# Re-cutting the head of a fused attention and Fourier kernel into ten segments, with GpSimd splits and two cycles for each of the last output tiles

## The chip, the cores and the metric

The kernel runs on one core of a Trainium2 chip. The metric is device time in microseconds (us), the median over runs of the whole kernel. Engines are named as the profile names them: PE (TensorE matmul) and PEld (its weight loads), DVE (VectorE), ACT (ScalarE), POOL (GpSimd), SP (SyncE, which here only issues DMAs).

## The reference

```python
def reference(A_x, A_wqkv, A_wo, B_x, B_dft_seq_re, B_dft_seq_im, B_dft_hid_re, B_dft_hid_im, gate_w):
    x = A_x                                              # (1, 2048, 640), 32 heads of 20
    g = _sigmoid((x * gate_w).sum(-1, keepdims=True))
    # a: attention
    qkv = (x @ wqkv).reshape(B, S, 3, H, Dh).transpose(2, 0, 3, 1, 4)
    q, k, v = qkv[0], qkv[1], qkv[2]
    scores = jnp.einsum("bhqd,bhkd->bhqk", q, k) * (Dh ** -0.5)
    a = jnp.einsum("bhqk,bhkd->bhqd", _softmax(scores), v) ... @ wo
    # b: real part of a DFT over hidden, then over sequence
    ar = jnp.einsum("bsd,ed->bse", x, dft_hid_re)
    ai = jnp.einsum("bsd,ed->bse", x, dft_hid_im)
    b = jnp.einsum("ts,bse->bte", dft_seq_re, ar) - jnp.einsum("ts,bse->bte", dft_seq_im, ai)
    return g * a + (1 - g) * b
```

## The kernel before

Everything is float32. Matmuls run on pairs of a rounded part and a remainder: `split` writes the rounded copy with one engine and the remainder (a subtract) with another, and a product takes three matmuls (`three`). The schedule is written out by hand: instructions stand on each engine in the order in which the program makes them, and tiles rotate through fixed numbers of buffers (five PSUM banks `ps` from `bank()`, five `pair_tile`s, three `raw_tile`s, three `part_tile`s). Stores are collected in a list and issued on SP by `flush(keep)`, which leaves the `keep` youngest for later.

**Head.** First come the projections. 40 q/k tiles (`qk_tile(c, t)`: 15 matmuls of 512 columns into one bank, a split from PSUM into a pair tile by ACT and DVE, and a store of 512 KB to DRAM) and the v tiles; then 32 of the q/k tiles, eight column blocks of four, with **segments** between them. A segment (`segment(i, steps)`, before the first tile of each block, eight in all) interleaves two other jobs:

- one hidden tile (`hid_tile`): one block of the DFT over the hidden dimension, 15 yields of two 64-row matmuls that run beside each other in the two halves of the array, into the banks `yp0` and `yp1`, then read by ACT (L357) and DVE (L358) and stored to `a_scr`;
- five score steps (`run_s`, `s_mm`, L167): per step two matmuls (two heads) of 512 scores, each followed by a DVE maximum (L169). The softmax needs the row maxima ahead of the exponentials; a head start of `LEAD = 41` steps is made here: eight segments of five steps, and one step at the end. After step 31 the first unit's maxima are gathered (`max_nm`), and after step 33 they are transposed (`max_chain`, L201).

Inside a segment each step is followed by three hidden yields.

**Main loop.** 256 cycles, each of which follows the string `ORDER`: eight scores `e` (L844, then an ACT exponential, L846), eight scores `m` for the maxima 41 steps ahead, 15 places `F` for fill, and at the end a burst `B` of 16 attention-times-v matmuls (L518) for the two key tiles of this cycle. The fill is a chain of generators, and `goals` says how far it is to be at each place: first the hidden tiles that the head has not made (64 less `HEAD`, so 56, one per cycle, L349), then 56 units of the DFT over the sequence, three cycles each (L599), then `out_tile`, the output product over the first four of five blocks of `wo` for the 16 row tiles, two halves each, one half per cycle (L670). That fills 56 + 168 + 32 = 256 cycles. The maxima run out 41 steps (ten cycles) before the end.

GpSimd makes the splits of the main loop, combines transfers, scales and adds the DFT result `y` to the output (`add`, L686 and L687), and normalises the attention output. Its `load_pre(tt)` brings a row tile of the attention output for `out_tile`. `LAST` holds what is loaded in the last ten steps: the fifth block of the first eight row tiles (`load_o4`) and the part of it that is known for the other eight (`load_old`).

**Tail.** After the last burst the last unit's attention output is normalised: `spread`, four `recip`, a product, four DMAs (`move`), `split_last`. Meanwhile `short_row(tt)` adds the fifth block for row tiles 0 to 7: six matmuls, a DVE or ACT+POOL addition per half, and the store of the row tile. After `split_last` the same is done for tiles 8 to 15.

Of the kernel before, what the change touches and what calls it, by code (L numbers as in the profile page):

```python
# [11 lines left out]
R = mybir.dt.float32r  # L12
AF = mybir.ActivationFunctionType
ALU = mybir.AluOpType
# [4 lines left out]
P = 128  # L19
S = 2048  # L20
D = 640
H = 32
DH = 20
ND = D // P
# [14 lines left out]

LEAD = 41  # L40

HEAD = 8

# [11 lines left out]


LONG = (0, 0, 0, 0, 0, 0, 0)
FULL = 0  # L60
PRE = range(FULL, NS)
UNITS = len(PRODUCTS) * HT

# [3 lines left out]
def f32(ap):  # L67
    return ap.bitcast(F32)
# [3 lines left out]
def mix_kernel(ctx: ExitStack, tc: tile.TileContext, xa, wqk, wb, cdft, wo, out):  # L72
    nc = tc.nc
    pe, act, dve, pool, sp = nc.tensor, nc.scalar, nc.vector, nc.gpsimd, nc.sync
# [16 lines left out]
    y_scr = dram.tile([NS, P, D], F32, name="y_scr")  # L91
    r_scr = dram.tile([NU, 4, 512], F32, name="r_scr")
    l_scr = dram.tile([NU, 4, 512], F32, name="l_scr")
    o_scr = dram.tile([D, S], F32, name="o_scr")
# [10 lines left out]
    ngate = const.tile([P, NS], F32, name="ngate")  # L105

    def split(dst1, dst2, src, e1, e2):
        if e1 is act:
            act.activation(dst1, src, AF.Copy)  # L109
        else:  # L110
            e1.tensor_copy(dst1, src)  # L111
        e2.tensor_tensor(dst2, src, f32(dst1), op=ALU.subtract)  # L112

    def three(ps, st1, st2, mv1, mv2, first, last):
        pe.matmul(ps, st1, mv1, start=first, stop=False)  # L115
        pe.matmul(ps, st1, mv2, start=False, stop=False)  # L116
        pe.matmul(ps, st2, mv1, start=False, stop=last)  # L117
# [3 lines left out]
    def bank():  # L121
        return ps_w.tile([P, 512], F32, name=f"ps{next(turn) % 5}")

    def pair_tile():
        return work.tile([P, 2, 512], F32, name="p", bufs=5)

    def raw_tile():
        return work.tile([P, 1024], F32, name="raw", bufs=3)

    def part_tile():  # L130
        return work.tile([P, 2, 1024], R, name="part", bufs=3)
# [21 lines left out]
    def at_step(i, fn):  # L153
        later.setdefault(i, []).append(fn)
# [103 lines left out]
    def idle(n):  # L258
        ps = bank()
        for _ in range(n):  # L260
            pe.matmul(ps, zeros[:, :P], zeros, start=True, stop=True)
# [27 lines left out]

        return finish  # L290

    stores = []

    def flush(keep=0):
        while len(stores) > keep:
            sp.dma_start(*stores.pop(0))

    def qk_tile(c, t):
        w = wt[c]
        ps = bank()  # L300
        x1, x2 = xs[0][t], xs[1][t]
        for d in range(ND):
            if (c, t) == (0, 0) and d > 0:
                if d == 1:
                    idle(3)
                pe.matmul(ps, w[:, 0, d], x1[:, d], start=False, stop=False)
                pe.matmul(ps, w[:, 1, d], x1[:, d], start=False, stop=False)
                pe.matmul(ps, w[:, 0, d], x2[:, d], start=False, stop=d == ND - 1)
            else:
                three(ps, w[:, 0, d], w[:, 1, d], x1[:, d], x2[:, d], d == 0, d == ND - 1)  # L310
        st = pair_tile()
        split(st[:, 0].bitcast(R), st[:, 1].bitcast(R), ps, act, dve)
        stores.append((qk_scr[:, t, c * P : (c + 1) * P].rearrange("z p c -> p z c"), st))
        flush(2)

    def mm_b(j, s, ps, n):
        w = wt["b", j]
# [46 lines left out]
    def segment(i, steps):  # L364
        def read_out(read, args):
            read()
            stores.append(args)

        tile_ = hid_tile(i, read_out)
        left = 3 * ND  # L370
        for k in range(steps):
            run_s(step + 1)
            for _ in range(left // (steps - k)):
                next(tile_)
                left -= 1

    step = 0

    def run_s(upto):
        nonlocal step  # L380
        while step < upto:
            s_step(step)
            step += 1
# [22 lines left out]
    for s in range(12, 16, 2):  # L406
        v_pair(0, s)
    fin()
    hid_done = 0
    order = [1, ND + 1, 2, ND + 2, 3, ND + 3, 4, ND + 4]  # L410
    for s in range(0, NS, 2):
        v_pair(1, s)
# [8 lines left out]
    for n, c in enumerate(order):  # L421
        for t in range(4):
            m = 4 * n + t
            if m % 4 == 0 and hid_done < HEAD:
                segment(hid_done, 5)
                hid_done += 1
            qk_tile(c, t)
            if t == 1:
                if n + 1 < len(order):
                    fin()  # L430
                if n + 2 < len(order):
                    fin = load_wqk(order[n + 2])
# [135 lines left out]
    signs = {}  # L568
    st = {(th * HT + t, hf): 0 for th in range(2) for t in range(HT) for hf in range(2)}
# [73 lines left out]
    def load_o4():  # L643
        raw = raw_tile()[:, : (HT - FULL) * P]
        sp.dma_start(raw, o_scr[(ND - 1) * P :, FULL * P : HT * P])
        at_step(total - 4, functools.partial(finish_o4, raw))

    def finish_o4(raw):
        o = part_tile()[:, :, : (HT - FULL) * P]
        split(o[:, 0], o[:, 1], raw, pool, pool)  # L650
        for t in range(FULL, HT):
            o4[t] = o[:, :, (t - FULL) * P : (t - FULL + 1) * P]

# [79 lines left out]
    ops = {}  # L733


    def make_sel():
# [3 lines left out]
            pool.tensor_copy(sel[:, 32 * j : 32 * j + 32], ident[:, c : c + 1].to_broadcast([P, 32]))  # L740
        chain.append(sel)

    total = 32 * NU
    LAST = {total - 10: load_o4, total - 9: load_old}
    done = 0
    goals = {}
    def read_later(read, args):
        extras.append((now[0], read))
        at_step(now[0] + 2, functools.partial(sp.dma_start, *args))

    HID = 4 * NS - HEAD
    fills = itertools.chain(*(hid_tile(HEAD + g, read_later) for g in range(HID)), itertools.chain.from_iterable(dft_step(g) for g in range(NS * UNITS)),
                            itertools.chain.from_iterable(out_tile(tt, hf) for tt in PRE for hf in range(2)))
# [5 lines left out]
    first = start // 4  # L759
    last = total // 4 - 1  # L760
    cycles = [(c, c + 1, 3 * ND) for c in range(HID)]
    edge = [first]
    for u in range(UNITS):
        k, t = LONG[u // HT], u % HT
        edge.append(edge[-1] + 3 + k * (t + 1) // HT - k * t // HT)
    cycles += [(edge[u], edge[u + 1], 3 * NS) for u in range(UNITS)]
    cycles += [(edge[-1] + u, edge[-1] + u + 1, 3 * (ND - 1)) for u in range(2 * len(PRE))]
    assert cycles[-1][1] <= last + 1
    at_goal = 0
    for c0, c1, count in cycles:  # L770
# [4 lines left out]
            at_goal += share  # L775

    for k, tt in enumerate(PRE):
        i = 4 * (edge[-1] + 2 * k)

        def load(tt=tt, i=i):  # L780
            at_step(i - 6, load_pre(tt))

        at_step(i - 11, load)
# [24 lines left out]
    def end(i):  # L808
        if i % 4 == 2:
            c = i // 4  # L810
            if c + HEAD in (NS, 2 * NS):
                at_step(i + 2, load_wb(3 + (c + HEAD) // NS, pool, pool))
            if c in (HID - 18, HID - 17, HID - 16):
# [5 lines left out]
            if c in (HID - 7, HID - 5, HID - 3):  # L819
                at_step(i + 4, load_c((c - HID + 7) // 2))  # L820
        if i in LAST:
            LAST[i]()

# [52 lines left out]
            fn()  # L876


    def out_half(tt, hf, y, ops, add, shared=False):
        ps = bank()[:, :HE]  # L880
        for k, (o1, o2, d) in enumerate(ops):
            w = wos[d, hf]
            three(ps, o1, o2, w[:, 0], w[:, 1], k == 0, k == len(ops) - 1)
        ye = y[:, hf * HE : (hf + 1) * HE]
        g = gate[:, tt : tt + 1]
        if shared:
            m = apool[0].tile([P, HE], F32, name="m", bufs=2)
            act.activation(m, ps, AF.Copy, scale=g)
            pool.tensor_tensor(ye, ye, m, op=ALU.add if add else ALU.subtract)
        else:  # L890
            dve.scalar_tensor_tensor(ye, ps, g, ye, op0=ALU.mult, op1=ALU.add if add else ALU.subtract)  # L891

    def short_row(tt, shared=False):
        for hf in range(2):
            out_half(tt, hf, yo[tt], [(o4[tt][:, 0], o4[tt][:, 1], ND - 1)], True, shared and hf == 1)
        sp.dma_start(out[tt * P : (tt + 1) * P, :], yo[tt])

    sel, o, rb = chain

# [9 lines left out]
    def move():  # L909
        for qc in range(2):  # L910
            for h in range(2):
                j = 2 * qc + h
                r = OLD + DH * h
                sp.dma_start(tip[0][r : r + DH, 512 * qc : 512 * qc + 512], o[32 * j : 32 * j + DH, :])  # L914

    def split_last():
        p = part_tile()
        for qc in range(2):
            c = slice(512 * qc, 512 * qc + 512)
            split(p[:, 0, c], p[:, 1, c], tip[0][:, c], act, dve)  # L920
        for t in range(HT):
            o4[HT + t] = p[:, :, t * P : (t + 1) * P]

    flush()
    short = list(range(FULL, HT))
    short_row(short[0])
    sums = spread()
    recip(sums, 0)
    for k, tt in enumerate(short[1:]):
        short_row(tt, k < 6)  # L930
        if k < 3:
            recip(sums, k + 1)
        if k == 3:
            dve.tensor_tensor(o, o, rb, op=ALU.mult)  # L934
            move()
    split_last()
    for tt in range(HT, NS):
        short_row(tt, False)

# [34 lines left out]
```

## Time and profile before

| | us |
|---|---|
| median of three runs | 1891.3 (1890.16 to 1892.07) |
| the profiled execution | 1889.33 |
| its span, first to last instruction | 1887.5 |
| head with segments | about 106 to 268 |
| hidden tiles in the main loop | 268 to 620 |
| DFT over the sequence | 620 to 1685 |
| output tiles | 1685 to 1862 |
| tail | 1862 to 1887.5 |

The stage borders are read from the matmul timeline. A row of the timeline gives start, duration, engine, line of the kernel, operation, tiles, shape and count; a bracket at its end holds the idle time of the engine before it and what ended it. A row of the waits gives the waiting instruction, what it waited for, total us, times, and the longest. A row of the groups ends in busy us, mean ns, idle time before. Back-to-back instructions overlap in the timeline (a matmul's end is modelled, and an exponential's 0.6 us contains the start of the next), so a pace is read from starts.

### The profile page before, as it was taken

The page shows a single profiled execution, that of the slowest core. Times are in us where ns is not written, and L with a number is a line of the kernel's source. Part 1 is how long each engine was busy: PE and PEld are TensorE (multiplying, and loading weights), DVE is VectorE, ACT ScalarE, POOL GpSimd, SP SyncE. Part 2 cuts the span into 40 slices and gives each one's busy share as a digit, 9 for nine tenths or more (in the row PEclk, how much of TensorE's full clock was granted, in tenths as well). Part 3 has the DMA queues.
Part 4 walks back from the last instruction along what each step waited for, and adds up shares of the span by engine and source line. Part 5 has one row for each costly group of instructions (what it writes and reads, how often), then busy time and mean ns, then how long its engine had stood idle before and what let it go on. Part 6 is the DMA issues. An engine that isn't in the chain of part 4 may idle for free. (4 is left out here: it accounts for less than half of the span.)

```text
span 1887.5 us, 44579 instructions
## 1 busy us (share of the span) xinstructions
PE 1875.0 (99%) x17477; PEld 1359.6 (72%) x17477; DVE 1471.1 (78%) x2448; ACT 1219.1 (65%) x2351; POOL 1007.0 (53%) x875
## 2 busy tenths in 40 slices
PE   9999999999999999999999999999999999999998
PEld 8987777676767676777767676777767676766666
DVE  4145469898989888888888888888888888889954
ACT  4221147777777676676767676766767676677784
POOL 1200001010035798466699899867779989634443
PEclk9999999999999999999999999999999999999999
DMA  7843341221415574636567576646485747342224
GB/s 232 179 135 133 123 148 48 65 72 50 120 45 155 167 230 148 169 119 180 175 172 243 164 250 189 170 145 185 135 250 192 217 161 213 120 114 62 61 56 151
DMA packets 174468, 280.50 MB, mean 149 GB/s; under 512 B 44095, under 2 KB 106559, under 8 KB 174259
## 3 DMA queue, kind: packets, MB, share of 16 engines
q1 hardware_dynamic: 173299, 275.69, 48.1%
q0 software_dynamic: 960, 1.97, 0.5%
q8 instruction: 137, 2.24, 0.5%
q14 instruction: 72, 0.59, 0.1%
HBM read 213.37 MB, written 63.52 MB: 147 GB/s over the span
## 5 line engine op out<-in xcount | busy, mean ns | idle before, releaser
L169 DVE TENSOR_REDUCE mx<-ps 128x1 f32<-128x512 f32 x2048 | 1294.0, 683 | 174.6 <-PE ps L167 153.8
L846 ACT ACTIVATE p<-ps 128x512 f32<-128x512 f32 x2048 | 1086.9, 599 | 432.7 <-PE ps L167 226.2
L167 PE MATMUL ps<-kst,qst 60*128 60x512 f32 x2048 | 790.2, 415 | 2.8 <-DVE p L112 0.5
L844 PE MATMUL ps<-qst,kst 62*128 62x512 f32 x2048 | 699.5, 413 | 0.2
L599 PE MATMUL yp<-x,part 64*128 64x320 f32 x5376 | 644.9, 307 | 0.0
L599 PEld LDWEIGHTS yp<-x,part 64*128 64x128 f32 x5376 | 580.1, 186 | 7.3
L518 PE MATMUL av<-p,v 128*21 128x512 f32 x4096 | 490.3, 596 | 0.0
L844 PEld LDWEIGHTS ps<-qst,kst 62*128 62x128 f32 x2048 | 336.2, 185 | 198.4 <-DVE mx L169 182.4
L167 PEld LDWEIGHTS ps<-kst,qst 60*128 60x128 f32 x2048 | 372.3, 184 | 22.7 <-DVE mx L169 9.8
L112 POOL TENSOR_TENSOR part<-raw,part 128x1024 fp32r<-128x1024 f32 (+1 forms) x129 | 290.3, 2250 | 10.3
L518 PEld LDWEIGHTS av<-p,v 128*21 128x21 f32 x4096 | 98.1, 100 | 225.6 <-issue 223.4
L349 PE MATMUL yp<-wb,x 64*128 64x320 f32 x1920 | 239.1, 308 | 0.0
L111 POOL CAST part<-raw 128x1024 fp32r<-128x1024 f32 (+1 forms) x129 | 127.1, 985 | 165.3 <-PE yp L599 154.9
L349 PEld LDWEIGHTS yp<-wb,x 64*128 64x128 f32 x1920 | 207.5, 186 | 4.0 <-DVE raw L358 0.2
L475 POOL TENSOR_TENSOR raw<-raw,raw 128x1024 f32<-128x1024 f32 x77 | 185.4, 2408 | 27.8 <-DMA raw<-in_cdft 22.2
L548 POOL TENSOR_TENSOR o<-o,rb 128x512 f32<-128x512 f32 x31 | 40.2, 1296 | 181.4 <-DMA rb<-r_scr 145.9
L111 POOL CAST wb<-raw 128x966 fp32r<-128x966 f32 (+1 forms) x4 | 3.4, 857 | 223.5 <-PE yp L349 223.5
L112 DVE TENSOR_TENSOR p<-ps,p 128x512 fp32r<-128x512 f32 x40 | 27.4, 690 | 92.5 <-ACT p L109 92.5
L670 PE MATMUL yp<-x,part 64*128 64x320 f32 x768 | 95.1, 309 | 0.0
L115 PE MATMUL ps<-x,part 128*128 128x512 f32 (+1 forms) x228 | 89.3, 392 | 2.6 <-ACT part L109 2.5
L112 POOL TENSOR_TENSOR x<-araw,x 128x320 fp32r<-128x320 f32 x96 | 83.8, 873 | 7.7
L117 PE MATMUL ps<-x,part 128*128 128x512 f32 (+1 forms) x228 | 87.8, 385 | 0.0
(80 smaller groups left out, 1174.7 us busy)
## 6 DMA issues: line engine op xcount, KB each, us to landing
raw<-in_cdft SPq DMA_DIRECT2D x192, 512.0 KB
araw<-a_scr SPq DMA_DIRECT2D x176, 160.0 KB
qk_scr<-p SPq DMA_DIRECT2D x40, 512.0 KB
kst<-qk_scr SPq DMA_DIRECT2D x90, 160.0 KB
qst<-qk_scr SPq DMA_DIRECT2D x90, 160.0 KB
a_scr<-raw SPq DMA_DIRECT2D x64, 160.0 KB
yt<-y_scr SPq DMA_DIRECT2D x64, 160.0 KB
y_scr<-yt SPq DMA_DIRECT2D x64, 160.0 KB
```

The source lines that it names most:

```text
L111: e1.tensor_copy(dst1, src)
L112: e2.tensor_tensor(dst2, src, f32(dst1), op=ALU.subtract)
L115: pe.matmul(ps, st1, mv1, start=first, stop=False)
L167: pe.matmul(ps, q[b : b + KROWS, qt * P : (qt + 1) * P], k[b : b + KROWS, kc * 512 : (kc + 1) * 512], start=True, stop=True)
L169: return lambda: dve.tensor_reduce(mx[n][:, h, qt, kc : kc + 1], ps, axis=AX.X, op=ALU.max)
L349: pe.matmul(yp[h][:, :HE], xs[xz][t][r, d, cs], w[r, wz, d, :HE], start=d == 0 and z == 0, stop=d == ND - 1 and z == 2)
L475: pool.tensor_tensor(raws[0], raws[0], raws[1], op=ALU.add if PRODUCTS[n][0][1][0] > 0 else ALU.subtract)
L518: pe.matmul(av[32 * j : 32 * j + DH + 1, :], v[:, kt, h * (DH + 1) : (h + 1) * (DH + 1)], pp[qc][:, h, :], start=kt == 0, stop=kt == NS - 1)
L599: pe.matmul(yp[h][:, :HE], c[r, cz, cs], a[r, az], start=s == 0 and z == 0, stop=s == NS - 1 and z == 2)
L670: pe.matmul(yp[h][:, :HE], o[r, oz, d], wos[d, hf][r, wz], start=d == 0 and z == 0, stop=d == ND - 2 and z == 2)
L844: pe.matmul(pt, k[b : b + KROWS + 2, kt * P : (kt + 1) * P], q[b : b + KROWS + 2, qc * 512 : (qc + 1) * 512], start=True, stop=True)
L846: act.activation(pts[n, kt, qc][:, h], pt, AF.Exp, scale=float(DH) ** -0.5)
```

## The change

`HEAD` goes from 8 to 10, and `segment` is called with four steps instead of five, before every third q/k tile instead of every fourth; `FILL` puts no hidden yields behind the first step, eight behind the second, seven behind the third and none behind the fourth. From the first segment on, `qk_tile` copies its bank out with ACT into half of a pair tile, GpSimd makes both parts of the split from there, and one store is kept back instead of two. In the main loop 54 hidden tiles remain. `FULL = 1` takes row tile 0 out of the output fill; 30 halves remain, and the last four (`SLOW`) get two cycles each, so that 54 + 168 + 26 + 8 = 256. Row tile 0 is made in the tail with all five blocks (`full_half`, 15 matmuls a half), its attention rows loaded eight steps before the end (`load_o`) and split on GpSimd two steps before the end, its `y` loaded and scaled there. Its short row goes.

```diff
-HEAD = 8
+FILL = {4: (0, 8, 7, 0)}
+HEAD = 10
...
-FULL = 0
+FULL = 1
+SLOW = 4
...
 def qk_tile(c, t):
...
+        if hid_done:
+            if not halves:
+                raw = pair_tile()
+                halves.extend((raw[:, 1], raw[:, 0]))
+            raw = halves.pop()
+            act.activation(raw, ps, AF.Copy)
         st = pair_tile()
-        split(st[:, 0].bitcast(R), st[:, 1].bitcast(R), ps, act, dve)
+        st1, st2 = st[:, 0].bitcast(R), st[:, 1].bitcast(R)
+        if hid_done:
+            split(st1, st2, raw, pool, pool)
+        else:
+            split(st1, st2, ps, act, dve)
         stores.append((qk_scr[:, t, c * P : (c + 1) * P].rearrange("z p c -> p z c"), st))
-        flush(2)
+        flush(1 if hid_done else 2)
...
 def segment(i, steps):
...
-        left = 3 * ND
-        for k in range(steps):
+        for n in FILL[steps]:
             run_s(step + 1)
-            for _ in range(left // (steps - k)):
+            for _ in range(n):
                 next(tile_)
-                left -= 1
...
-            if m % 4 == 0 and hid_done < HEAD:
-                segment(hid_done, 5)
+            if m % 3 == 0 and hid_done < HEAD:
+                segment(hid_done, 4)
                 hid_done += 1
...
+    def load_o(tt):
+        raw = raw_tile()[:, : ND * P].rearrange("p (d c) -> p d c", d=ND)
+        sp.dma_start(raw, o_scr[:, tt * P : (tt + 1) * P].rearrange("(d p) c -> p d c", p=P))
+
+        def finish():
+            o = part_tile().rearrange("p z c -> p (z c)")[:, : 2 * ND * P].rearrange("p (z d c) -> p z d c", z=2, d=ND)
+            split(o[:, 0], o[:, 1], raw, pool, pool)
+            ops[tt] = o
+
+        return finish
...
-    LAST = {total - 10: load_o4, total - 9: load_old}
+    LAST = {total - 10: load_o4, total - 9: load_old, total - 8: lambda: fins.append(load_o(0)), total - 2: lambda: fins.pop()()}
...
-    cycles += [(edge[-1] + u, edge[-1] + u + 1, 3 * (ND - 1)) for u in range(2 * len(PRE))]
+    at_tile = edge[-1]
+    for u in range(2 * len(PRE)):
+        n = 2 if u >= 2 * len(PRE) - SLOW else 1
+        cycles.append((at_tile, at_tile + n, 3 * (ND - 1)))
+        tiles.append(at_tile)
+        at_tile += n
...
+    def load_y(tt):
+        ys[tt] = pair_tile().rearrange("p z c -> p (z c)")[:, :D]
+        sp.dma_start(ys[tt], y_scr[tt])
+
+    def scale_y(tt):
+        pool.tensor_scalar(ys[tt], ys[tt], ngate[:, tt : tt + 1], 1.0, op0=ALU.mult, op1=ALU.mult)
...
+    def full_half(tt, hf):
+        o = ops[tt]
+        out_half(tt, hf, ys[tt], [(o[:, 0, d], o[:, 1, d], d) for d in range(ND)], signs[tt, hf] > 0)
+        if hf:
+            sp.dma_start(out[tt * P : (tt + 1) * P, :], ys.pop(tt))
...
     flush()
+    for tt in range(FULL):
+        load_y(tt)
     short = list(range(FULL, HT))
...
             move()
+            scale_y(0)
+    full_half(0, 0)
     split_last()
+    full_half(0, 1)
     for tt in range(HT, NS):
         short_row(tt, False)
```

More of the change, by code (lines that the diff above doesn't have):

```diff
@@ L290, in load_wb @@
         return finish
-    stores = []
+    stores, halves, hid_done = [], [], 0
     def flush(keep=0):
@@ L408, in mix_kernel @@
     fin()
-    hid_done = 0
     order = [1, ND + 1, 2, ND + 2, 3, ND + 3, 4, ND + 4]
@@ L741, in make_sel @@
         chain.append(sel)
+    def load_o(tt):
[6 more added lines that the diff above has]
+        return finish
     total = 32 * NU
-    LAST = {total - 10: load_o4, total - 9: load_old}
+    LAST = {total - 10: load_o4, total - 9: load_old, total - 8: lambda: fins.append(load_o(0)), total - 2: lambda: fins.pop()()}
     done = 0
-    goals = {}
+    goals, fins = {}, []
     def read_later(read, args):
@@ L761, in mix_kernel @@
     cycles = [(c, c + 1, 3 * ND) for c in range(HID)]
-    edge = [first]
+    edge, tiles = [first], []
     for u in range(UNITS):
@@ L777, in mix_kernel @@
     for k, tt in enumerate(PRE):
-        i = 4 * (edge[-1] + 2 * k)
+        i = 4 * tiles[2 * k]
         def load(tt=tt, i=i):
@@ L876, in mix_kernel @@
             fn()
+    ys = {}
+    def load_y(tt):
[3 more added lines that the diff above has]
+        pool.tensor_scalar(ys[tt], ys[tt], ngate[:, tt : tt + 1], 1.0, op0=ALU.mult, op1=ALU.mult)
     def out_half(tt, hf, y, ops, add, shared=False):
```

## The prediction

> **What bounds the kernel now.** I read the page's busy times first, then the span cut by stage, then inside each stage what the matmul engine (PE) waits for, and last the timelines of one segment, one cycle and the tail.
>
> ```profile
> PE 1875.0 (99%) x17477; PEld 1359.6 (72%) x17477; DVE 1471.1 (78%) x2448; ACT 1219.1 (65%) x2351; POOL 1007.0 (53%) x875
> ```
> ```profile
> 106.10:268.20 162.10, 158.75 (x854) 123.82 (x853) 86.47 (x142) 32.87 (x58) 0.00 (x0) 1.00 0.37 131
> 268.20:620.20 352.00, 352.00 (x3483) 250.59 (x3481) 316.63 (x536) 259.60 (x512) 56.68 (x59) 1.00 0.29 84
> ...
> 1822.70:1862.40 39.70, 39.70 (x400) 24.15 (x398) 10.03 (x19) 33.45 (x67) 22.58 (x27) 1.00 0.29 85
> 1862.40:1887.50 25.10, 17.84 (x100) 15.84 (x98) 17.30 (x33) 5.03 (x9) 5.87 (x7) 0.93 0.56 216
> ```
> Columns of the second fence: window, length, then PE, weight load, DVE, ACT and POOL busy, granted clock, DMA. The rows are the segments with the q/k tiles, the 56 hidden cycles, the cycles without maxima, and the tail. PE sets the pace until the tail, but 99% is a modelled figure: in the segments it hides short waits. POOL does nothing there. The profiled execution took 1889.33 us, 1.83 more than its span and 1.97 under the median of 1891.3; I sum changes against 1889.33 and carry the difference to the median. Timings of this kernel can tell about 0.2% (3.8 us) from no change.
>
> **1. Segments: ten of four steps.** The waits of PE's weight loads in that window:
>
> ```profile
> PEld ps L167 <- DVE mx L169: 9.8, 24, 0.4
> PEld ps L167 <- issue: 3.1, 9, 0.4
> PEld ps L115 <- issue: 1.5, 8, 0.2
> ```
> Together 14.4 us. One segment shows how they arise:
>
> ```profile
> 143.88 0.50 PE L167 MATMUL ps<-kst,qst 60*128 60x512 f32 x2
> 144.22 0.61 PE L349 MATMUL yp<-wb,x 64*128 64x320 f32 x6
> 144.66 0.40 PE L167 MATMUL ps<-kst,qst 60*128 60x512 f32 x2
> 144.90 0.60 PE L349 MATMUL yp<-wb,x 64*128 64x320 f32 x6
> 145.37 1.09 PE L167 MATMUL ps<-kst,qst 60*128 60x512 f32 x2
> ...
> 149.23 0.50 PE L115 MATMUL ps<-x,part 128*128 128x512 f32 x1
> ```
> ```profile
> 145.23 6.06 DVE L169 TENSOR_REDUCE mx<-ps 128x1 f32<-128x512 f32 x10
> ```
> A step's two matmuls cost PE 0.24 us (144.66 to 144.90), the first step 0.34; three hidden pairs cost 0.44 (144.22 to 144.66), 0.147 each, 2.2 for a tile's fifteen. Unhindered, a segment takes 0.34 + 4 x 0.24 + 2.2 = 3.5; it takes 5.35. The ten maxima come out 0.60 apart (6.06 for ten, 0.66 for one), five banks hold their scores, and the sixth matmul (begun 1.09 - 0.49 after 145.37) waits for the first maximum. That maximum starts late, too: DVE first has the split of the last q/k tile.
>
> Now 8 maxima per segment, and no q/k split on DVE. Walk one, from 0: steps one and two to 0.58; eight pairs to 1.76; step three to 2.00; seven pairs to 3.03; step four to 3.27. Maxima end near 1.2, 1.8, 2.4, 3.0 (first score at 0.5, 0.66 for its maximum, then one per 0.60). PE needs the first at 1.9, the second at 3.0, the third at 3.1, and the q/k tile behind needs the fourth at 3.27: all are there, the last by 0.3. So the 14.4 goes, and two more hidden tiles cost 2 x 2.2 = 4.4; the 41 score steps are as many as before. **Head: -10.0.** Bounds: a wait of 0.2 left in each of ten segments gives -8; -11 if the transpose at step 33, whose operand is now made a segment earlier, stops waiting as well.
>
> **2. Splits on GpSimd.** Each of 32 tiles exchanges a DVE subtract for a GpSimd cast and subtract; ACT still does one pass out of PSUM.
>
> ```profile
> L112 POOL TENSOR_TENSOR part<-raw,part 128x512 fp32r<-128x512 f32 x10 | 12.9, 1293 | 0.8
> ...
> L111 POOL CAST part<-raw 128x512 fp32r<-128x512 f32 x9 | 5.5, 610 | 0.7 <-PE ps L844 0.7
> ```
> ```profile
> L112 DVE TENSOR_TENSOR p<-ps,p 128x512 fp32r<-128x512 f32 x32 | 22.1, 691 | 74.6 <-ACT p L109 74.6
> ```
> ```profile
> 140.55 0.60 ACT L109 ACTIVATE p<-ps 128x512 fp32r<-128x512 f32 x1 [2.21 <-PE ps L117]
> 143.99 0.60 ACT L109 ACTIVATE p<-ps 128x512 fp32r<-128x512 f32 x1 [2.84 <-PE ps L117]
> ```
> A tile leaves PE every 3.44 us; GpSimd needs 0.61 + 1.29 = 1.90 of it. The bank is free after ACT's 0.60, sooner than now, so PE waits for nothing new. What comes later is the store on SP's queue, by about 1.2; behind it wait the load of the next column block's weights, used four tiles later, and, at the end of the head, the load of v, which has a whole cycle before its first burst. The pair tiles turn faster: three per two q/k tiles out of five buffers, so one returns after about 3.3 tiles, over 11 us plus a segment, against 0.6 + 1.9 plus the store:
>
> ```profile
> 135.03 10.66 SPq L296 DMA_DIRECT2D qk_scr<-p  x4
> ```
> ```profile
> 148.00:149.00 1.00, 0.90 (x9) 0.65 (x7) 1.00 (x3) 0.00 (x0) 0.00 (x0) 1.00 0.00 0
> ```
> The fourth store's issue ends at 145.69 and DMA is still at 148: about 2.3. Cost taken: **0**; a late first exponential could cost 0 to 1.
>
> The Trainium skill, GPSIMD Engine Reference, section 3.1 Elementwise, speaks against this edit: elementwise arithmetic belongs on VectorE, a subtract takes GpSimd about twice as long. The trace agrees (1293 against 691 ns); by that rule the time rises only if the subtract is waited for, which is the third rival below.
>
> **3. Two hidden cycles become two output cycles.** Bursts (16 matmuls each) count the cycles:
>
> ```profile
> 268.20:620.20 352.00, 107.22 (x896) 21.31 (x896) 1.00 0.29 84
> ...
> 1684.90:1783.10 98.20, 30.63 (x256) 6.08 (x256) 1.00 0.28 78
> ```
> 56 cycles of 6.286, and 16 of 6.138. The total stays 256 cycles, so **-0.3**; the DFT stage keeps its 168, only shifted by two against the eight-cycle units, which I bound at -1 to +1.
>
> **4. The last eight cycles with half the fill.** They come after the last maxima.
>
> ```profile
> 1846.42:1851.16 4.74, 4.74 (x51) 2.98 (x49) 1.10 (x3) 4.03 (x9) 3.08 (x3) 1.00 0.80 245
> 1855.90:1860.40 4.50, 4.50 (x48) 2.83 (x46) 1.04 (x2) 3.78 (x9) 1.38 (x2) 1.00 0.00 0
> ```
> ```profile
> 1848.85 4.03 ACT L846 ACTIVATE p<-ps 128x512 f32<-128x512 f32 x8 [0.71 <-PE ps L844]
> ```
> ```profile
> 1846.08 0.40 PE L844 MATMUL ps<-qst,kst 62*128 62x512 f32 x2
> 1846.42 1.91 PE L518 MATMUL av<-p,v 128*21 128x512 f32 x16
> 1848.26 0.50 PE L844 MATMUL ps<-qst,kst 62*128 62x512 f32 x2
> ```
> Six pairs out of twelve leave each cycle: PE then needs 4.74 - 6 x 0.147 = 3.86, and ACT, at (4.03 - 0.60) / 7 = 0.49 per exponential, 3.92. Neither alone is the answer, for the burst stands in between: the score just ahead of it needs the bank of the third exponential (2 x 0.49 + 0.60 = 1.58 after the first begins, plus 0.06 as in the segment from maximum to matmul), then some 0.25 to the burst (the pair takes 0.34), 1.84 to the next score, 0.59 to its exponential: 4.32. Seven cycles x 0.42, and the very last, without scores at its end, 4.50 - 0.88 = 3.62: **-3.8**. Bounds: nothing, and -6.6 (ACT at 3.92 throughout).
>
> **5. The tail.** Tile 0 loses its short row and gets two halves of 15 matmuls.
>
> ```profile
> 1862.67 0.31 PE L116 MATMUL ps<-x,part 128*128 128x320 f32 x1
> 1862.82 0.31 PE L117 MATMUL ps<-x,part 128*128 128x320 f32 x1
> ```
> ```profile
> 1873.80 0.42 PE L115 MATMUL ps<-x,part 128*128 128x320 f32 x1 [2.50 <-ACT part L109]
> ```
> ```profile
> 1875.29 0.69 DVE L112 TENSOR_TENSOR part<-raw,part 128x512 fp32r<-128x512 f32 x1 [0.82 <-ACT part L109]
> 1875.90 1.46 DVE L891 SCALAR_TENSOR_TENSOR x<-ps,gate,x 128x320 f32<-128x320 f32 x3
> 1877.60 6.07 DVE L891 SCALAR_TENSOR_TENSOR x<-ps,gate,x 128x320 f32<-128x320 f32 x13 [0.23 <-PE ps L117]
> ```
> 15 x 0.147 = 2.2 per half. PE is free from 1871.3 (1873.80 - 2.50) to 1873.8 now, and 0.9 earlier without one short row: 4.4 of work ends near 1874.8, 1.0 into the last rows. But DVE sets the end: it is done with the split at 1875.98 and has 17 results of 0.46 instead of 16, until 1883.8; it ends at 1883.67 now. **+0.2**, bounds -0.5 and +2 (GpSimd's split of tile 0, or its load, late).
>
> Sum: -10.0 - 0.3 - 3.8 + 0.2 = -13.9, so 1875.4 as profiled and **1877.4** on the median.
>
> **Rivals.** (a) The last cycles gain nothing, because ACT is late in every loop: 1881.2. For it speaks that PE and ACT will need nearly the same (3.86 and 3.92), so that each hand-over between them shows; against, the 0.71 in which ACT now stands still each cycle. (b) ACT runs without a gap: 1874.6. (c) Slower, GpSimd on the path: the five pair tiles come back late, so that ACT, and behind it the bank, waits for GpSimd. Each tile then pays 0.61 + 1.29 - 0.69 = 1.21, together 38.7: 1916.1. It decides from 13.9 / 32 = 0.43 per tile; against it stand 11 us of return time for some 5 of use. (d) The segments stay bound by the maxima, since steps four and one have no pairs behind them: with today's 1.8 in each of ten, the head costs +8 instead of -10, 1895.4; half of it 1886.4. Against it the walk, whose smallest margin is 0.3. (e) The edits cancel within what can be measured.
>
> **Chances.** Forecast 0.70, (a) 0.10, (b) 0.05, (c) 0.04, (d) 0.04 in full and 0.04 by half, (e) 0.03. Faster: 0.70 + 0.10 + 0.05 + 0.04 = 0.89; same 0.03; slower 0.08. The range takes in (b) and (a) with the bounds of head and tail, 1873.5 to 1884.0; (c), (d), (e) and the forecast's own edge stay out, near 0.2.
>
> **What would show it.** Right: waits of score weight loads for maxima under 3 us in the head, 3.3 to 3.5 from a segment's first matmul to the next q/k matmul, cycles of about 4.3 before the tail, no halved clock in it, DVE busy to the end. Wrong: ACT in the head waiting for POOL, a segment above 4 us, cycles still at 4.7, or PE in the tail waiting for tile 0's split.

## The result and the profile after

The changed kernel takes 1883.6 us (median of six runs, 1881.85 to 1886.34) against 1890.59 for the kernel before (six runs): ratio 0.9962, interval 0.9952 to 0.9972, so 7.0 us faster where 13.9 were forecast. The interval does not contain 1, so the gain is real, though small. The profiled execution took 1884.27 us, 5.1 under the profiled execution of before.

The page's busy times, and the stages of the changed kernel (segments with q/k tiles, the 56 cycles that follow, the cycles without maxima from the 249th on, the tail; columns as in the prediction):

```profile
PE 1872.0 (99%) x17453; PEld 1356.7 (72%) x17453; DVE 1448.5 (77%) x2410; ACT 1220.4 (65%) x2353; POOL 1069.7 (57%) x936
```
```profile
105.60:262.70 157.10, 154.13 (x918) 124.09 (x918) 68.52 (x113) 34.98 (x63) 64.51 (x64) 1.00 0.39 136
262.70:614.00 351.30, 350.77 (x3467) 249.00 (x3469) 312.96 (x528) 256.95 (x506) 64.22 (x63) 1.00 0.31 91
1822.90:1854.90 32.00, 32.00 (x253) 16.89 (x252) 3.46 (x7) 27.54 (x56) 13.10 (x14) 1.00 0.33 88
1854.90:1882.50 27.60, 22.34 (x139) 18.60 (x138) 18.39 (x35) 6.69 (x13) 7.27 (x8) 0.96 0.53 203
```

Cut at the starts of the same matmuls in both traces, the time went as follows; the last column is what the forecast had for each stretch.

| stretch | before | after | change | forecast |
|---|---|---|---|---|
| start to first segment (nothing edited) | 106.11 | 105.57 | -0.5 | 0 |
| first segment to first burst | 162.10 | 157.10 | -5.0 | -10.0 |
| of it, the segments themselves | 42.72 | 36.76 | -6.0 | -10.0 |
| 224 cycles from the first burst | 1416.73 | 1418.07 | +1.3 | -0.3 |
| the next 24 cycles (the last of them is the first with half the fill) | 142.51 | 142.19 | -0.3 | -0.4 |
| the next seven cycles, to the last burst | 32.95 | 31.96 | -1.0 | -3.4 |
| last burst to the end | 27.14 | 27.57 | +0.4 | +0.2 |

The head gave half of its forecast, the last eight cycles a third (0.2 of the 24 cycles' 0.3 lies in the first of the eight). In the head, the scores' weight loads now wait for a maximum as follows, where the prediction shows 9.8 us in 24 waits:

```profile
PEld ps L170 <- DVE mx L172: 2.5, 3, 1.1
```
A segment that goes as forecast, and one that does not (timeline of PE, then of DVE; the segments begin at 148.64 and 133.49):

```profile
148.64 0.73 PE L170 MATMUL ps<-kst,qst 60*128 60x512 f32 x4
149.21 1.35 PE L362 MATMUL yp<-wb,x 64*128 64x320 f32 x16
150.38 0.41 PE L170 MATMUL ps<-kst,qst 60*128 60x512 f32 x2
150.62 1.21 PE L362 MATMUL yp<-wb,x 64*128 64x320 f32 x14
151.65 0.41 PE L170 MATMUL ps<-kst,qst 60*128 60x512 f32 x2
151.99 0.50 PE L118 MATMUL ps<-x,part 128*128 128x512 f32 x1
```
```profile
133.49 0.73 PE L170 MATMUL ps<-kst,qst 60*128 60x512 f32 x4
134.06 1.34 PE L362 MATMUL yp<-wb,x 64*128 64x320 f32 x16
135.24 0.40 PE L170 MATMUL ps<-kst,qst 60*128 60x512 f32 x1
136.34 0.49 PE L170 MATMUL ps<-kst,qst 60*128 60x512 f32 x1 [0.70 <-DVE mx L172]
...
138.13 0.50 PE L118 MATMUL ps<-x,part 128*128 128x512 f32 x1
```
```profile
134.85 0.82 DVE L115 TENSOR_TENSOR part<-raw,part 128x640 fp32r<-128x640 f32 x1 [9.16 <-ACT part L112]
135.60 3.67 DVE L172 TENSOR_REDUCE mx<-ps 128x1 f32<-128x512 f32 x6
...
149.17 3.68 DVE L172 TENSOR_REDUCE mx<-ps 128x1 f32<-128x512 f32 x6 [8.31 <-PE ps L170]
```
The first takes 3.35 us to the next q/k tile, and its maxima start 0.53 after its first matmul. The second takes 4.64: its maxima start 2.1 after its first matmul, behind the split of a weight block that itself waited for ACT, and the sixth score waits for the first maximum, as in the kernel before. Of the ten segments six take 3.35; the others take 3.53, 3.85 (the one with the transpose) and twice 4.64.

The first burst now waits for v, whose load SP issues behind the last store (SP's timeline, then PE's):

```profile
253.76 3.69 SPq L299 DMA_DIRECT2D qk_scr<-p  x2
257.50 1.52 SPq L520 DMA_DIRECT2D v<-v_scr  x1
```
```profile
262.68 0.63 PE L528 MATMUL av<-p,v 128*21 128x512 f32 x4 [1.22 <-DMA v<-v_scr]
```
A cycle near the end (ACT's timeline, PE's, and PE's weight loads):

```profile
1839.53 4.03 ACT L872 ACTIVATE p<-ps 128x512 f32<-128x512 f32 x8 [0.64 <-PE ps L870]
1844.20 4.03 ACT L872 ACTIVATE p<-ps 128x512 f32<-128x512 f32 x8 [0.64 <-PE ps L870]
```
```profile
1840.67 0.98 PE L870 MATMUL ps<-qst,kst 62*128 62x512 f32 x2
1841.58 2.09 PE L528 MATMUL av<-p,v 128*21 128x512 f32 x16
1843.61 0.50 PE L870 MATMUL ps<-qst,kst 62*128 62x512 f32 x2
```
```profile
1841.16 0.18 PEld L870 LDWEIGHTS ps<-qst,kst 62*128 62x128 f32 x1 [0.31 <-ACT p L872]
...
1842.46 0.29 PEld L528 LDWEIGHTS av<-p,v 128*21 128x21 f32 x6 [0.32 <-issue]
1843.60 0.18 PEld L870 LDWEIGHTS ps<-qst,kst 62*128 62x128 f32 x2 [0.85 <-issue]
```
The cycle is 4.66 us long, and ACT still stands still for 0.64 of it (0.71 before). The score ahead of the burst is held until an exponential has freed its bank (1841.16); 0.42 later the burst starts, 2.03 after that the next score.

### The profile page after: what moved, and what is told of

The parts are those of the page before. It is cut to its first block, busy times and chain, and to the rows that moved or that the text cites. A ratio compares the mean times of both kernels' runs of the same rounds, so it can differ in the third digit from the quotient of the medians.

```text
span 1882.5 us, 44546 instructions
## 1 busy us (share of the span) xinstructions
PE 1872.0 (99%) x17453; PEld 1356.7 (72%) x17453; DVE 1448.5 (77%) x2410; ACT 1220.4 (65%) x2353; POOL 1069.7 (57%) x936
## 5 line engine op out<-in xcount | busy, mean ns | idle before, releaser
L170 PE MATMUL ps<-kst,qst 60*128 60x512 f32 x2048 | 776.3, 413 | 1.5 <-DVE mx L172 1.4
L609 PEld LDWEIGHTS yp<-x,part 64*128 64x128 f32 x5376 | 580.2, 186 | 7.5
L170 PEld LDWEIGHTS ps<-kst,qst 60*128 60x128 f32 x2048 | 368.1, 184 | 15.1 <-issue 3.8
L362 PE MATMUL yp<-wb,x 64*128 64x320 f32 x1920 | 226.8, 307 | 0.5 <-ACT raw L370 0.4
L362 PEld LDWEIGHTS yp<-wb,x 64*128 64x128 f32 x1920 | 201.4, 186 | 5.2 <-ACT raw L370 0.7
L118 PE MATMUL ps<-x,part 128*128 128x512 f32 (+1 forms) x236 | 91.2, 387 | 0.3
L120 PE MATMUL ps<-x,part 128*128 128x512 f32 (+1 forms) x236 | 89.6, 380 | 0.0
L119 PE MATMUL ps<-x,part 128*128 128x512 f32 (+1 forms) x236 | 89.3, 378 | 0.0
L680 PEld LDWEIGHTS yp<-x,part 64*128 64x128 f32 x720 | 81.7, 186 | 3.0
```

The lines of the kernel that those rows point to most:

```text
L170: pe.matmul(ps, q[b : b + KROWS, qt * P : (qt + 1) * P], k[b : b + KROWS, kc * 512 : (kc + 1) * 512], start=True, stop=True)
L362: pe.matmul(yp[h][:, :HE], xs[xz][t][r, d, cs], w[r, wz, d, :HE], start=d == 0 and z == 0, stop=d == ND - 1 and z == 2)
L609: pe.matmul(yp[h][:, :HE], c[r, cz, cs], a[r, az], start=s == 0 and z == 0, stop=s == NS - 1 and z == 2)
L680: pe.matmul(yp[h][:, :HE], o[r, oz, d], wos[d, hf][r, wz], start=d == 0 and z == 0, stop=d == ND - 2 and z == 2)
```

## The experiments

The theory after this reading (A in each expectation): a segment is as long as DVE's lateness makes it; in the last cycles a loop of exponential, bank, score, burst, score sets the time, not the fill; and the load of v hangs on the last store. The rivals are in the expectations. All of these start from the changed kernel (1883.6) unless said otherwise; times are medians, ratios are against the kernel before. The runs were taken in several sessions, in which the median of the kernel before went from 1890.25 to 1890.91, so differences of half a microsecond between two medians say nothing.

**The splits back on ACT and DVE.**

```diff
-        if hid_done:
+        if False:
             if not halves:
...
-        if hid_done:
+        if False:
             split(st1, st2, raw, pool, pool)
...
-        flush(1 if hid_done else 2)
+        flush(2)
```


> The changed kernel with the q/k splits back on ACT and DVE (two stores kept back). Theory A (the splits on GpSimd are what lets the maxima of a segment start at once): DVE begins each segment with the split of the last q/k tile, the fourth maximum ends near 3.8 us instead of 3.0 and the q/k tile behind the segment waits: segments of 3.9 to 4.0 us instead of 3.35, +4 to +6 us over ten segments; the wait of the first burst for v (1.2 us) goes, so +3 to +5 us in all against the changed kernel. Theory B (the splits do nothing, the longer fill alone shortens the segments): segments stay at 3.35, and the time falls by the 1.2 us of the wait for v.

1888.61 us, ratio 0.9992 (0.9983 to 1.0001): 5.0 slower than the changed kernel. The segments add up to 40.49 instead of 36.76; five of the ten take 3.87. On DVE, in the one that begins at 150.00:

```profile
150.74 0.69 DVE L115 TENSOR_TENSOR p<-ps,p 128x512 fp32r<-128x512 f32 x1 [2.70 <-ACT p L112]
151.34 3.67 DVE L172 TENSOR_REDUCE mx<-ps 128x1 f32<-128x512 f32 x6
```
The split stands right ahead of the maxima, which start 1.34 after the segment's first matmul instead of 0.53. So theory A holds for the segments: work that GpSimd does more slowly is the part of the change that most of the gain hangs on. Its other half failed: no wait for v is left in this trace, but the stretch from the last step of the head to the first burst did not get shorter by 1.2, it got 1.0 longer.

**The weight split later.** Where a column block's weight split stood in front of a segment, it is made one tile later.

```diff
-            if t == 1:
+            if t == (2 if n % 3 == 1 else 1):
                 if n + 1 < len(order):
                     fin()
```


> The changed kernel with the split of the next weight block made one q/k tile later in the column blocks where it stood right in front of a segment. Theory A (two segments take 4.64 instead of 3.35 us because DVE has that split, which waits for ACT, ahead of the maxima): both fall to 3.35, -2.6 us in the head. Theory B (they are long for another reason, such as GpSimd being late or the pair tiles): they stay at 4.64, no change.

1881.2 us, ratio 0.9951 (0.9938 to 0.9963), 2.4 less. The segments add up to 34.16, 2.60 less, and both long ones are at 3.35. Here is DVE in the first of them, and the split behind it:

```profile
134.87 3.68 DVE L172 TENSOR_REDUCE mx<-ps 128x1 f32<-128x512 f32 x6 [8.33 <-PE ps L170]
...
142.77 0.82 DVE L115 TENSOR_TENSOR part<-raw,part 128x640 fp32r<-128x640 f32 x1 [2.64 <-ACT part L112]
```
That is theory A, to a tenth in the segments and within 0.2 in the median.

**v loaded earlier.**

```diff
             qk_tile(c, t)
+            if m == 28:
+                load_v(0)
...
-    load_v(0)
     apool = []
```


> The changed kernel with the first load of v issued three q/k tiles before the end of the head instead of behind the last store. Theory A (the first burst waits 1.2 us for v, because SP holds the load until GpSimd has made the last split): the wait goes, first burst 1.2 us earlier. Theory B (the burst would then wait as long for the exponentials): under 0.3 us.

1883.75 us, ratio 0.9964 (0.9952 to 0.9977): no change in the median. In its trace no wait for v is left, and the first burst comes 155.80 after the first segment instead of 157.10. But in the other kernels with the same head that stretch was 156.14, 155.90, 156.60 and 156.52: measured against 155.80, the wait costs between 0.1 and 1.3, 0.65 in the mean. The traces show the mechanism; its size in the median is below what the runs resolve.

**No slow output halves.** `SLOW = 0`, so that the last four cycles have no fill.

> The changed kernel with one cycle for each of the last four output halves, so that the last four cycles have no fill at all. Theory A (without maxima a cycle is held by the loop burst, score, exponential, bank, at 4.66 us, whatever the fill): four cycles of 4.74 and four near 4.6, within 0.7 us of the changed kernel. Theory B (the fill decides, down to ACT's 3.92): the empty cycles fall to 3.9 to 4.0, -2.4 to -2.8 us.

1884.15 us, ratio 0.9966 (0.9954 to 0.9978). ACT in cycles without any fill:

```profile
1843.03 4.03 ACT L872 ACTIVATE p<-ps 128x512 f32<-128x512 f32 x8 [0.64 <-PE ps L870]
1847.69 4.03 ACT L872 ACTIVATE p<-ps 128x512 f32<-128x512 f32 x8 [0.64 <-PE ps L870]
```
The cycle is 4.66 from start to start with nothing to fill, as with half the fill, and 4.74 with all of it. This is theory A: from half the fill down, the loop sets the cycle.

**The burst in two halves.**

```diff
+HALF = 16
...
+    LATE = (total - LEAD) // 4 + 1
...
-        for kt in (2 * c, 2 * c + 1):
+        for kt in (2 * c, 2 * c + 1)[c >= LATE :]:
...
+            if at_ == HALF and c >= LATE:
+                av_step(now[0], 2 * c // NS, 2 * c % NS)
```
Place 16 of `ORDER` is behind the fourth score `e`, and `LATE` is 246 here, so that ten cycles have the halves.

> The changed kernel; in the cycles without maxima the burst is made in two halves, the first key tile behind the fourth score and the second at the end. Theory A (a burst of 2.0 us in one piece starves ACT, which has five banks or 2.5 us of exponentials in front of it): cycles of 3.95 to 4.1 us instead of 4.66, -4 to -5 us over the last eight. Theory B (the halves wait for their exponentials instead, as a half needs younger ones): cycles stay at 4.5 or more, -1 us or less.

1891.51 us, ratio 1.0004 (0.9995 to 1.0012): 7.9 slower than the changed kernel. Neither theory had that, though B was right that the cycles stay above 4.5: they are 5.40 long. PE's weight loads over one half:

```profile
1840.80 0.12 PEld L529 LDWEIGHTS av<-p,v 128*21 128x21 f32 x4 [0.27 <-issue]
1841.42 0.13 PEld L529 LDWEIGHTS av<-p,v 128*21 128x21 f32 x4 [0.50 <-ACT p L873]
1842.39 0.18 PEld L871 LDWEIGHTS ps<-qst,kst 62*128 62x128 f32 x2 [0.85 <-issue]
```
A half waits 0.5 in its middle for an exponential, and the next score's weights come 0.85 after the half's last ones. So a half takes 1.59 of PE (1840.80 to 1842.39), and ACT stands still 0.64 behind each half instead of once a cycle. Theory B named the wait; that two stops a cycle would make the cycle longer was missed.

**The head alone.** The head of the changed kernel; `FULL = 0`, `SLOW = 0` and the old tail.

> The head of the changed kernel (ten segments, GpSimd splits) with the output tiles and the tail of the kernel before; the last two cycles have no fill. Theory A (the head gives 5 to 6 us, the last cycles and the tail next to nothing): -4 to -6.5 us against the kernel before. Theory B (the forecast, -10 for the head): -9 us or more.

1885.02 us, ratio 0.9969 (0.9956 to 0.9981), 5.9 under the kernel before, as theory A has it.

**The output part alone.** Old head, `FULL = 1`, `SLOW = 2`.

> The head of the kernel before, with row tile 0 made in the tail and two slow halves (two cycles each) instead of four, as 256 cycles then hold no more. Theory A (slow cycles 0.08 us shorter each, the last by 0.5, the tail 0.5 longer): within 1 us of the kernel before. Theory B (the forecast's 0.42 per slow cycle): -2 us or more.

1890.71 us, ratio 0.9996 (0.9988 to 1.0005): no change, as theory A has it. Nearly all of the gain is the head's.

**The three edits together** (later weight split, earlier v, the half bursts above).

> The changed kernel with the later weight split, the earlier load of v and the half bursts together. Theory A (they act in different places and add up): -2.6 - 1.2 - 4.5 = about -8 us against the changed kernel. Theory B (a gain in one place is given back at the next wait, above all in the tail): -5 us or less.

1888.18 us, ratio 0.9986 (0.9977 to 0.9995). Its head is 153.22 long, 3.9 less than the changed kernel's, and its last seven cycles 37.80, 5.8 more. Theory A fails; the half bursts spoil it.

**Halves of older keys.** The same two places in the last eight cycles, but each half takes the key tile that lies half a cycle further back. `HALF` is 16 as above, `LATE` is 248, and the last half of all stands behind the loop.

```diff
+    LATE = total // 4 - 8
...
-        for kt in (2 * c, 2 * c + 1):
+        for kt in (2 * c, 2 * c + 1)[: 1 if c >= LATE else 2]:
...
+            if at_ == HALF and c > LATE:
+                av_step(now[0], (2 * c - 1) // NS, (2 * c - 1) % NS)
...
+    av_step(now[0], NU - 1, NS - 1)
```


> The changed kernel; in the last eight cycles the burst is made in two halves, each of the key tile that lies half a cycle further back (behind the fourth score the second tile of the cycle before, at the end the first tile of this one), so that no half needs an exponential younger than the one whose bank the score ahead of it waited for. Theory A (a half costs PE 0.9 to 1.0 us when its exponentials are done, and ACT has 2.5 us in front of it): ACT no longer stands still, cycles of 4.0 to 4.2 us instead of 4.66, -3.5 to -4.5 us against the changed kernel. Theory B (the end of every burst costs PE about 0.85 us before the next score can start, so two halves cost more than one whole): cycles of 4.5 us or more, no gain.

1879.98 us, ratio 0.9943 (0.9931 to 0.9956), 3.6 less than the changed kernel. PE over one half, and ACT over five cycles:

```profile
1837.11 1.06 PE L529 MATMUL av<-p,v 128*21 128x512 f32 x8
1838.10 0.49 PE L871 MATMUL ps<-qst,kst 62*128 62x512 f32 x1
```
```profile
1829.60 20.57 ACT L873 ACTIVATE p<-ps 128x512 f32<-128x512 f32 x39
```
A half takes 0.99 instead of 1.59, the cycle is 4.19, and ACT's row no longer breaks. Within the row short stops are left: one exponential begins 0.48 to 0.50 after the other, but every fourth 0.64 to 0.65 after it, behind a half. The stop thus costs about 0.17 twice a cycle; in the changed kernel, where one interval of 1.31 stands in each cycle, it is about 0.83. This is theory A, and it shows the loop: no work was taken out, only the wait for a young exponential went and most of the starved stretch. Halves and older keys came together here; a whole burst of older keys was not run, so how much the halving adds is not shown.

**The version that the experiments point to:** later weight split, earlier v, halves of older keys.

> The changed kernel with the later weight split, the earlier load of v and the older halves together. Theory A: -2.6 for the split, about -0.6 for v (its wait was 0.3 to 1.5 us in the kernels with this head), and what the older halves give alone; near 1877 us if they give 4. Theory B (gains of the last cycles are given back in the tail): 1880 us or more.

1877.67 us (1876.59 to 1878.55), ratio 0.9930 (0.9916 to 0.9943): 12.9 under the kernel before, 5.9 under the changed one. The head is 153.22 long and the last seven cycles 29.09, as theory A has it.

## Why the prediction was right or wrong

The direction, the place of the gain and the mechanism of the segments were right; the size was off by half, mostly in two terms, the segments and the last eight cycles. The time lies inside the range, 0.4 under its upper edge, and some of that is luck: the terms as the traces have them add up to -5.1, which would have made 1885.5, outside it. Of the signs that were to show the forecast wrong, two appeared: segments above 4 us (two of ten), and cycles still near 4.7 (4.66).

**Segments, -10.0 forecast, -6.0 measured.** The walk gave 3.27 per segment and six of ten take 3.35. What failed is the sentence that no split stands on DVE ahead of the maxima. It counted the q/k splits and not the weight block's split: made behind the second tile of each column block, it never stood in front of a segment with one segment per four tiles, and twice does with one per three. That is 2 x 1.29 (shown by the later split). The transpose left 0.5 and not nothing, the segment of 3.53 has a split of `wb` on DVE until 120.51, ahead of its maxima, and all ten take 0.08 more than the walk, because step four costs 0.34 instead of 0.24 where the q/k tile follows (151.65 to 151.99). These make up the 4.1 between 10 x 3.27 and 36.76. That last 0.08 is no wait for a maximum: in the six segments of 3.35 the maximum that the q/k tile needs had ended 0.32 before its weights were loaded, so the margin of 0.3 was right. One reading was wrong: of the 14.4 us taken for waits, the rows put down to "issue" are gaps that stay, for the scores 3.8 us in 11 places in the changed head. That cost nothing, since the walk gives the same -10.0 (42.72 less 32.7).

**GpSimd's splits at cost 0.** Right for PE, ACT and the pair tiles: of the head's waits none for POOL shows. What DVE gained by it had no number of its own in the forecast; by the first experiment it is 5.0, of which 3.7 in the segments. The page of the Trainium skill that speaks against it, GPSIMD Engine Reference, section 3.1 Elementwise, is right on the price of one operation (1.29 against 0.69 us here), but its rule does not give this kernel's time, since no engine waits for the split itself; only the last store, and the load of v behind it, come later. Wrong was "a whole cycle before its first burst" for v: the load's issue alone took SP 1.52 us where it took 0.46 in the kernel before, and the first burst, which waited for it, came 5.2 after the issue began and 1.2 after PE was free.

**Two cycles exchanged, -0.3.** By bursts, the 16 output cycles are again 6.14 long. The +1.3 in the table holds one cycle of 7.40, in which ACT waits 1.13 for a buffer that GpSimd holds until a load lands. Cycles of 6.6 to 7.1 stood near the same place in most of the other kernels, the one with the old head among them, and in none of the kernel before's profiled run; what brings them on is open.

**The last eight cycles, -3.8 forecast, about -1.2 measured** (-1.0 to the last burst, and -0.2 in the cycle ahead of them). The loop was the right one, and two of its terms were too small: from the score ahead of the burst to the burst 0.42 and not 0.25 (the score's weights are loaded only when its bank is free), and the burst 2.03 and not 1.84: its last four weight loads start at 1842.63 in the trace, just behind the end of the sixth exponential at 1842.58. With the terms as measured the loop is 1.63 + 0.42 + 2.03 + 0.59 = 4.67, and the gain is close to what the forecast called rival (a), which had none.

**The tail, +0.2.** Right within its bounds: +0.4, DVE busy to the end of its work, no halved clock in the last rows, where the kernel before had a granted clock of 0.51 from 1874.0 to 1877.5:

```profile
1871.07 0.55 DVE L926 SCALAR_TENSOR_TENSOR p<-ps,gate,p 128x320 f32<-128x320 f32 x1
1871.53 7.42 DVE L926 SCALAR_TENSOR_TENSOR x<-ps,gate,x 128x320 f32<-128x320 f32 x16
```
```profile
1870.00:1879.00 9.00, 7.33 (x47) 6.64 (x45) 8.49 (x18) 0.43 (x1) 0.00 (x0) 1.00 0.77 306
```
Seventeen results follow the split without a gap, at a granted clock of 1.00. (The 0.96 of the tail's row comes from 1880.2 on, when PE has no matmul left.)

Against these -5.1 in the profiled executions, the medians differ by 7.0. The stretch ahead of the first segment, which no edit touches, took 105.3 to 108.3 us in the ten runs, so a single profile can't settle the last two microseconds.

## What to carry to other kernels

When an interleaving period changes from four to three, list what stands in front of each new place on every engine's queue: a job that never met the critical group before can meet it now. Moving an operation to a slower engine pays if the slower engine's result is waited for by nobody and the faster one's queue is what the critical group stands in. In a loop through several engines, lowering the load of one of them gives nothing until the hand-overs are counted; here, halves of the burst that take data half a cycle older removed most of the wait with no work taken out.

## What was unexpected of the hardware

After a burst of column-tiled matmuls the next score's weights were loaded 0.85 us after the burst's last ones, for eight matmuls as for sixteen. It looks like a fixed price of each burst, but it is not one: a half of older keys takes 0.99 in all, so two take 1.98, and a whole burst takes 1.84 in the kernel before. Cutting a burst in two costs about 0.14; what made the half bursts slow was the wait in them.

A row of the timeline can hide short stops. The 39 exponentials in one row of 20.57 us come at (20.57 - 0.60) / 38 = 0.526 in the mean, but three of four intervals are 0.48 to 0.50, as in the runs of eight, and the fourth is 0.64 to 0.65. Read from single starts, an exponential takes ACT 0.48, so eight take 3.83 and not the 3.92 of the prediction. That the cycle stays at 4.19 is thus not the pace of ACT. The score behind a half did not wait for its bank either, which an exponential had freed 0.46 earlier (at 1837.63, the score began at 1838.10); that PE's own work sets the 4.19 is likely, and no run here shows it.
